# Attention with pooled queries and a three-way max FFN on one core: weights converted in two DVE passes ahead of the first FFN, key sums of eight units on PE, twelve score buffers

## The chip, the cores and the metric

The kernel runs on one core of one Trainium2 chip. The metric is the device time of one execution in microseconds (us), as the median of several runs. The engines named here are PE (matrix products), DVE (vector), ACT (scalar, activations and copies), POOL (elementwise) and SP (which issues nearly all DMAs). Each works through its own instructions strictly in the order in which the program puts them.

## The reference, cut to what matters

```python
q_pool = q.reshape(B, H, S // 2, 2, D).mean(axis=3)       # 8 x 8 heads, 1152 -> 576 queries, D = 64
scores = scale * np.matmul(q_pool, k.transpose(0, 1, 3, 2))  # 576 x 1152
scores = scores - np.max(scores, axis=-1, keepdims=True)
attn = np.exp(scores)
attn = attn / (np.sum(attn, axis=-1, keepdims=True) + 1e-09)
x = np.matmul(attn, v)                    # then to 4608 tokens x 512
h = np.maximum(np.maximum(x @ w1, x @ w2), x @ w3)        # 512 -> 768
out = h @ w_out                                           # 768 -> 512
```

q, k and v are float32. The four weight matrices arrive as float64, which the kernel reads as pairs of 32-bit words.

## The kernel before, in words

**Units.** A unit `d` (0 to 63) is one half (288) of the pooled queries of two heads; two units share one load of keys, queries and values. For each of nine blocks of 128 keys, PE makes the scores of both heads (`pqk`, from two parts of each operand: `qq`, `kc`), ACT copies them into a score buffer (`s`, three blocks in each), and DVE keeps the running maximum over blocks (`acc`). PE turns the maxima (`pmt`), DVE reduces them (`m`), PE spreads them (`pmb`), DVE subtracts them from the scores in six instructions, ACT takes the exponentials in six, and PE multiplies by the values (`pav`). ACT copies the product to `xr`, once per unit. A unit needs three score buffers; there are six.

**Key sums.** POOL adds the nine blocks of a unit's exponentials with eight instructions into `ksum` (lines 643 and 645). For the first 16 units six small PE products turn `ksum` into columns (`psum`, line 704), DVE inverts them, PE spreads the result (line 719) and DVE scales `xr` (line 728). Later units use another form (lines 687 to 697).

**FFN.** The tokens go in nine chunks, eight of 512 and one of 576 split in two. A chunk has 18 first-layer weight tiles in six groups of three. For each, PE makes twelve products (`ph`, line 935); ACT and DVE keep the maximum of three (`hm`), which is split into a high and a low part (`h_hi`, `h_lo`). The second layer (`po`, line 990) has 72 products. The chunk's work is mixed into that of the following units.

**Weights.** Each of 24 weight tiles (18 of the first layer, 6 of the second) is made from 128 x 512 float64 numbers: a DMA brings them to one of the two halves of `w64` (line 820); ACT scales the high words (line 835); four DVE passes rebuild the float32 value and the rest that it lacks (lines 838, 843, 848, 851); ACT makes the high part (line 862) and two more passes the low part (lines 865, 868). Even tiles go in one piece and leave the last two passes to POOL; odd tiles go in two pieces of 256 columns and have all six passes on DVE. The load of tile j waits until tile j-2 is done. During chunk 0 these tiles feed its products directly, and each of the 18 is stored to `w_split` in HBM (line 881), from which the later chunks fetch it (line 895). There are four tiles of room (`w`), so the first four conversions come among units 1 to 4, the fifth only when chunk 0 has used the first, and the second layer's six at the end of chunk 0.

**Order.** A planner in the program (`arrange`) puts all steps in order: it follows its own cost of every step, and among those ready on an engine it takes the one with the lowest urgency, from the tables `RANK` (by kind) and `NUDGE` (single steps of units and chunks below 20). Two PSUM buffers called `ff` serve `ph`, `po`, `psum`, the first eight units' `pav` and the conversion.

Of the kernel before, what the change touches and what calls it, by code (L numbers as in the profile page):

```python
# [18 lines left out]
P = 128  # L19
D = 64  # L20
# [16 lines left out]
    "qk": -364.0396,  # L37
    "cp": -126.5549,
    "mx": -318.2574,
    "rows": -969.9796,  # L40
    "red": -172.0313,
    "bc": -345.8464,
    "sub": 215.1752,
    "exp": 196.9402,
    "keys": -671.9276,
    "av": 14.8431,
    "xcopy": -516.1778,
    "psum": 398.4083,
    "eps": 343.2889,
    "inv": 357.0576,  # L50
    "xm": -706.0274,
    "load": 386.6538,
    "prep": 638.9001,
    "move": 1290.4425,
    "split": 283.1141,
    "ffn": -33.8173,
    "rate": 1.047,
    "mm": 49.0387,
    "fetch": 603.0832,
    "evac": -724.5554,  # L60
    "hhigh": 1228.3483,
    "hlow": -714.7034,
    "conv": 648.8915,
    "rate0": 4.5084,
    "first_qk": -97.1625,
    "first_cp": -630.79,
    "first_mx": 212.4188,
    "first_sub": 204.5779,
    "first_exp": 244.1512,
    "first_keys": -1118.9276,  # L70
    "first_av": 141.406,
    "first_xcopy": -152.0387,
    "first_psum": 65.359,
    "first_inv": 141.5566,
    "first_xm": 829.3378,
    "first_load": -197.5173,
    "first_prep": 180.1798,
    "first_move": -1436.3679,
    "first_split": 375.0794,
# [94 lines left out]
EARLY = 16  # L174
SPLIT = 8
IDLE = 0
APART = 0
SWITCH = 0.2


# [894 lines left out]
```

## Time and profile before

| What | us |
|---|---|
| three runs, median (lowest to highest) | 1474.91 (1472.44 to 1477.5) |
| the profiled execution, its own time | 1472.96 |
| its span, first to last instruction | 1471.1 |
| PE busy | 1398.0 |
| POOL busy | 1079.1 |
| DVE busy | 1044.0 |
| ACT busy | 902.5 |

A row of instructions in the profile reads: line, engine, operation, output and inputs by tile name, shapes, count, then busy time and the mean nanoseconds of one. A window row reads: from and to in us, its length, then the busy time of PE, PEld (weight loads, which run beside products), DVE, ACT and POOL with instruction counts, then the TensorE clock that was granted as a share of full speed, the mean busy share of the 16 DMA engines, and GB/s. A timeline row begins with its start and its length in us. SPq is the queue of SP.

### The profile page before, as it was taken

To read this page: it belongs to the slowest core of one execution; us is meant where nothing else is said; L and a number is where in the kernel's file an instruction comes from. 1 tells how busy PE (TensorE), PEld (TensorE's weight loads), DVE (VectorE), ACT (ScalarE), POOL (GpSimd) and SP (SyncE) were. 2 spreads that over 40 slices of the span, in tenths; PEclk is the share of its full clock that TensorE was granted. 3 is DMA by queue.
4 is the path that set the end of the run, shared out by engine and by line. 5 is a ranking of instruction groups with operands and counts; after the bars stand their busy time and mean duration, and the time that the engine had idled before them with its cause. 6 is when DMAs were issued, how large, how long until landed. Compare 5 with 4: busy or idle time off the path is not lost.

```text
span 1471.1 us, 24704 instructions
## 1 busy us (share of the span) xinstructions
PE 1398.0 (95%) x8704; PEld 1098.5 (75%) x8704; DVE 1044.0 (71%) x1441; ACT 902.5 (61%) x1464; POOL 1079.1 (73%) x835
## 2 busy tenths in 40 slices
PE   4888999898899999999999999999999999999999
PEld 4566677675677878777777777777777777878999
DVE  3897789898877767777688778777787768861110
ACT  3776776567666666567566766666766757651211
POOL 1897975889868878679888878888787978772210
PEclk9988999998899999999999999999999999999999
DMA  6675456576456656565567556664566556414441
GB/s 181 169 203 147 122 153 207 184 206 194 118 151 185 201 155 182 168 181 148 148 192 203 152 145 191 182 182 134 163 189 184 149 148 185 144 69 162 149 161 59
DMA packets 114762, 240.71 MB, mean 164 GB/s; under 512 B 15440, under 2 KB 75216, under 8 KB 114640
## 3 DMA queue, kind: packets, MB, share of 16 engines
q1 hardware_dynamic: 114064, 238.55, 55.8%
q8 instruction: 70, 1.15, 0.3%
q10 hardware_dynamic: 576, 0.59, 0.2%
q14 instruction: 52, 0.43, 0.1%
HBM read 144.70 MB, written 18.87 MB: 111 GB/s over the span
## 4 chain that ended last, share of the span: by engine, by line
PE 75%; DVE 10%; DMA 4%; ACT 4%; issue 4%; POOL 2%; SPq 1%; ACTq 0%; DVEq 0%; POOLq 0%
PE ph L935 28%; PE pav L673 14%; PE po L990 10%; PE pqk L542 9%; PE pqk L543 8%; DVE s L624 3%; DVE acc L557 3%; DMA kraw<-in_kT_dram 2%; PE pmt L593 2%; PE psum L687 2%; PE pmb L609 2%; POOL ksum L645 1%; ACT s L548 1%; DVE w L848 1%; DVE w L843 1%
## 5 line engine op out<-in xcount | busy, mean ns | idle before, releaser
L645 POOL TENSOR_TENSOR ksum<-ksum,s 128x576 f32<-128x576 f32 x448 | 638.2, 1425 | 26.1 <-ACT s L630 3.5
L935 PE MATMUL ph<-xh,w 128*128 128x512 f32 (+2 forms) x1440 | 464.3, 376 | 2.7 <-DVE w L868 1.3
L548 ACT COPY s<-pqk 128x576 f32<-128x576 f32 x576 | 362.4, 639 | 103.4 <-PE pqk L543 97.8
L624 DVE TENSOR_TENSOR s<-s,pmb 128x693 f32<-128x693 f32 (+1 forms) x384 | 395.1, 1049 | 39.5 <-PE pmb L609 38.3
L542 PE MATMUL pqk<-qq,kc 128*128 128x288 f32 x1152 | 357.9, 326 | 56.1 <-DVE acc L557 30.7
L557 DVE TENSOR_TENSOR acc<-acc,pqk 128x576 f32<-128x576 f32 x448 | 335.3, 749 | 82.8 <-ACT s L548 78.1
L630 ACT ACTIVATE s<-s 128x693 f32<-128x693 f32 (+1 forms) x384 | 352.5, 933 | 41.9 <-DVE s L624 38.6
L543 PE MATMUL pqk<-qq,kc 128*128 128x288 f32 x1152 | 332.3, 303 | 0.0
L542 PEld LDWEIGHTS pqk<-qq,kc 128*128 128x128 f32 x1152 | 225.6, 196 | 113.7 <-DVE acc L557 44.5
L673 PE MATMUL pav<-s,v 128*64 128x288 f32 x2304 | 306.8, 418 | 1.3 <-ACT s L630 1.0
L935 PEld LDWEIGHTS ph<-xh,w 128*128 128x128 f32 x1440 | 263.1, 188 | 41.4 <-ACT xr L682 1.8
L935 PE MATMUL ph<-xl,w 128*128 128x512 f32 (+2 forms) x720 | 268.3, 373 | 0.0
L673 PEld LDWEIGHTS pav<-s,v 128*64 128x64 f32 x2304 | 165.2, 140 | 119.3 <-issue 16.6
L543 PEld LDWEIGHTS pqk<-qq,kc 128*128 128x128 f32 x1152 | 227.5, 197 | 10.4
L643 POOL TENSOR_TENSOR ksum<-s 128x576 f32<-128x576 f32 x64 | 92.0, 1437 | 107.8 <-ACT s L630 104.8
L956 DVE TENSOR_TENSOR hm<-hm,ph 128x512 f32<-128x512 f32 (+2 forms) x120 | 75.8, 631 | 126.8 <-PE ph L935 124.8
L966 POOL TENSOR_TENSOR h_lo<-hm,h_hi 128x512 fp32r<-128x512 f32 (+2 forms) x60 | 70.6, 1176 | 126.1 <-ACT h_hi L963 123.6
L935 PEld LDWEIGHTS ph<-xl,w 128*128 128x128 f32 x720 | 135.8, 189 | 11.5
L438 POOL TENSOR_TENSOR kraw<-kraw 128x1152 fp32r<-128x1152 f32 x31 | 82.8, 2670 | 63.1 <-DMA qraw<-in_qT_dram 26.6
L599 DVE TENSOR_REDUCE m<-pmt 116x3 f32<-116x384 f32 (+1 forms) x128 | 61.3, 488 | 89.9 <-PE pmt L593 89.8
L682 ACT COPY xr<-pav 128x288 f32<-128x288 f32 x64 | 25.5, 399 | 147.0 <-PE pav L673 146.9
L694 DVE RECIPROCAL rs<-rs 128x288 f32<-128x288 f32 (+1 forms) x64 | 96.5, 1507 | 17.7 <-ACT rs L691 17.3
(57 smaller groups left out, 1293.6 us busy)
## 6 DMA issues: line engine op xcount, KB each, us to landing
w<-w_split SPq DMA_DIRECT2D x144, 512.0 KB, 3.6
kc<-kraw SPq DMA_DIRECT2D x384, 96.0 KB, 2.2
qq<-qraw SPq DMA_DIRECT2D x252, 144.0 KB, 3.3
v<-in_vr_dram SPq DMA_DIRECT2D x32, 576.0 KB, 3.8
kraw<-in_kT_dram SPq DMA_DIRECT2D x31, 576.0 KB, 6.0
qraw<-in_qT_dram SPq DMA_DIRECT2D x31, 576.0 KB, 4.0
w<-in_win_dram SPq DMA_DIRECT2D x18, 512.0 KB, 5.9
w_split<-w SPq DMA_DIRECT2D x18, 512.0 KB, 5.5
```

Of the source, the lines that this page charges most:

```text
L542: nc.tensor.matmul(ps[:, h - hs[0], :QH], w, qq[:, 0, h], start=True, stop=False)
L543: nc.tensor.matmul(ps[:, h - hs[0], :QH], w, qq[:, 1, h], start=False, stop=True)
L548: nc.scalar.copy(o.s[kk // 3][:, kk % 3, slice(*hs)], o.ps[kk, hs][:, :, :QH])
L557: nc.vector.tensor_tensor(acc, acc, ps, op=ALU.max)
L624: nc.vector.tensor_tensor(s, s, o.pb[h][:, None, :w].broadcast_to([P, 3, w]), op=ALU.subtract)
L630: nc.scalar.activation(s, s, AF.Exp, scale=SCALE)
L643: vec[e].tensor_tensor(o.ksum, o.s[0][:, 0], x, op=ALU.add)
L645: vec[e].tensor_tensor(o.ksum, o.ksum, x, op=ALU.add)
L673: nc.tensor.matmul(o.pav[64 * h : 64 * h + 64, :QH], pr.v[:, kk, h], o.s[kk // 3][:, kk % 3, h], start=(kk == 0), stop=(kk == NK - 1),)
L694: nc.vector.reciprocal(o.rs, o.rs)
L935: nc.tensor.matmul(t.ps[:, : hi - lo], w[:, a, kk], xx[:, kk, lo:hi], start=(kk == 0 and i == 0), stop=(kk == 3 and i == 2),)
L990: nc.tensor.matmul(t.ps[:, : hi - lo], ww[:, kk, ms], hh[:, kk, lo:hi], start=(kk == 0 and i == 0), stop=(kk == 5 and i == 2),)
```

## The change

1. **Conversion.** Only `shift` and `sign` stay on DVE, and every tile goes in one piece. The low words become a count of units of the last place in a new ACT pass (`units_of`), POOL adds it to the value as an integer (`carry`), ACT makes the high part, POOL the low part (`low`). Nothing of the odd tiles' last passes is left on DVE.
2. **Place.** All 24 conversions are planned at the head of chunk 0, not inside it. The 18 first-layer tiles are all stored to `w_split`, through the same four `w` buffers, and chunk 0 fetches them from there like the other chunks. Its first fetches wait until all 18 high parts are made.
3. **Key sums.** For units 0 to 7 POOL's eight adds go. PE multiplies each exponential block by a 128 x 32 block of ones into one of four 32-column tiles (18 products), ACT copies the result (`kt`), and three small products with a selection matrix give the columns.
4. **Buffers.** Eight score buffers in place of six, and units 0 to 7 put their last three blocks into four buffers that later hold the FFN's `h`, so that up to four units are held at once.
5. **Tables.** `RANK` and `NUDGE` have other numbers throughout; the scratch space of the DMA queue is set to 1024 bytes.

```diff
-    "sub": 215.1752,
+    "sub": 3142.3735,
...
-    "conv": 648.8915,
+    "conv": 1789.7153,
...
-    spool = ctx.enter_context(tc.tile_pool(name="spool", bufs=6))
+    spool = ctx.enter_context(tc.tile_pool(name="spool", bufs=THIRDS))
...
-    hpool = ctx.enter_context(tc.tile_pool(name="hpool", bufs=1))
+    hpool = ctx.enter_context(tc.tile_pool(name="hpool", bufs=4))
...
-                if kk % 3 == 0 and old2:
-                    after += [old2.avs[kk + 2], old2.sums[kk + 1]]
+                if kk % 3 == 0:
+                    lent = d < LENT and kk == 6
+                    seq = homes[lent]
+                    past = len(seq) - (4 if lent else THIRDS)
+                    if past >= 0:
+                        was, last_kk = seq[past]
+                        after += [was.avs[last_kk], was.sums[last_kk - 1] if was.sums else chain[was.d]]
+                    seq.append((o, kk + 2))
...
-        for kk in range(1, NK):
+        for kk in range(1, NK) if d >= SUMS else ():
...
+        def columns_keys(e):
+            o.psm = ps_ff.tile([P, 512], F32, tag="ff", name=f"psum{d}")
+            for kk in range(NK):
+                for h in range(2):
+                    t = 2 * h + kk % 2
+                    nc.tensor.matmul(
+                        o.psm[32 * t : 32 * t + 32, :QH],
+                        ones[:, :32],
+                        o.s[kk // 3][:, kk % 3, h],
+                        start=kk < 2,
+                        stop=kk >= NK - 2,
+                        tile_position=(0, 32 * t),
+                    )
+
+        def sums_copy(e):
+            o.kt = small.tile([P, QH], F32, tag="kt", name=f"kt{d}", bufs=1)
+            nc.scalar.copy(o.kt, o.psm[:, :QH])
+
+        def sums_turn(e):
+            for i in range(3):
+                nc.tensor.matmul(
+                    o.psm[:96, QH + 2 * i : QH + 2 * i + 2], o.kt[:, 96 * i : 96 * i + 96], sel, start=True, stop=True
+                )
...
-            wide = j % 2 == 1
-            m = DM // 2 if wide else DM
+            m = DM
...
-                def power(e):
-                    nc.vector.tensor_scalar(q.m.bitcast(U32), q.f, 0xFF800000, None, op0=ALU.bitwise_and)
-
-                def rest(e):
-                    nc.vector.scalar_tensor_tensor(
-                        q.low.bitcast(F32), q.low, 2.0**-52, q.m, op0=ALU.mult, op1=ALU.mult
-                    )
+                def units_of(e):
+                    nc.scalar.activation(o.low, o.low, AF.Copy, scale=2.0**-29)
+
+                def carry(e):
+                    nc.gpsimd.tensor_tensor(o.f, o.f, o.low, op=ALU.add)
...
-                a = cstep([dve(m)], power, [a])
-                a = cstep([dve(m)], rest, [a], give=None if wide else "ff")
-                end = dve(m) if wide else pool(m)
-                c = cstep([end], low, [c, a])
-                return cstep([end], total, [c, a], give="ff" if wide else None)
+                a = cstep([dve(m)], sign, [a], give="ff")
+                c = cstep([act(m)], units_of, [loaded])
+                a = cstep([pool(m)], carry, [a, c])
+                c = cstep([("act", 0.09 + m / 1200)], high, [a] + gone + highs[-1:])
+                highs.append(c)
+                return cstep([pool(m)], low, [c, a])
...
-            gone = wuse[j - 4] if 4 <= j < NG else []
+            gone = [stored[j - 4]] if 4 <= j < NG else []
...
-            if b:
-                fetch(g)
-            else:
+            fetch(g)
+
+        base = NG * b
+        if b == 0:
+            for g in range(NG + 6):
                 convert(g)
```

Three places show what this does to the order. The first is DVE at the conversion of weight tile 5, which before stands between units 10 and 11 (`w64` with two numbers after it is a PSUM piece, `w0_5` the finished tile):

```order
L838 TENSOR_SCALAR w64_105<-w64_5_0_1947 128x256
L843 SCALAR_TENSOR_TENSOR w64_5_0_1947<-w64_5_0_1947,w64_105 128x256
L838 TENSOR_SCALAR w64_105<-w64_5_256_1952 128x256
L848 TENSOR_SCALAR w64_5_0_1947<-w64_5_0_1947 128x256
L843 SCALAR_TENSOR_TENSOR w64_5_256_1952<-w64_5_256_1952,w64_105 128x256
L851 SCALAR_TENSOR_TENSOR w64_105<-w64_105,w64_5_0_1947 128x256
L848 TENSOR_SCALAR w64_5_256_1952<-w64_5_256_1952 128x256
L865 TENSOR_TENSOR w64_5_0_1947<-w64_5_0_1947,w0_5_1957 128x256
L851 SCALAR_TENSOR_TENSOR w64_105<-w64_105,w64_5_256_1952 128x256
L868 TENSOR_TENSOR w0_5_1957<-w64_5_0_1947,w64_105 128x256
L865 TENSOR_TENSOR w64_5_256_1952<-w64_5_256_1952,w0_5_1957 128x256
L599 TENSOR_REDUCE m10_0_1987<-pmt10_0_1967 116x3
```

In the change tiles 7 and 8 stand on DVE between units 4 and 5, before unit 4's maxima are reduced:

```order
L574 TENSOR_TENSOR acc4_831<-acc4_831,pqk4_7_928 128x576
L777 TENSOR_TENSOR xr_108<-xr_108,psum2_834 128x288
L890 TENSOR_SCALAR w64_107<-w64_7_0_960 128x512
L895 SCALAR_TENSOR_TENSOR w64_107<-w64_7_0_960,w64_107 128x512
L574 TENSOR_TENSOR acc4_831<-acc4_831,pqk4_8_955 128x576
L890 TENSOR_SCALAR w64_107<-w64_8_0_1000 128x512
L895 SCALAR_TENSOR_TENSOR w64_107<-w64_8_0_1000,w64_107 128x512
L622 TENSOR_REDUCE m4_0_1023<-pmt4_0_1005 116x3
```

So DVE has two rows for a tile where it had twelve (or four for an even tile), and they have moved from the units beside chunk 0 to the units before it. By the place of the rows, tile 17 is made about unit 9.

The second place is PE around the sums of unit 3. Before, one row of six small products stands among unit 5's scores:

```order
L673 MATMUL pav4_1007<-s4_0_732,v2_635 64x288 x6
L542 MATMUL pqk5_5_1019<-qq2_1_728,kc2_1_587 128x288
L543 MATMUL pqk5_5_1019<-qq2_1_728,kc2_1_587 128x288
L704 MATMUL psum3_1025<-ones_99,ksum3_823 96x1 x6
L542 MATMUL pqk5_6_1039<-qq2_1_728,kc2_2_663 128x288
```

In the change:

```order
L556 MATMUL pqk5_0_963<-qq2_1_739,kc2_0_433 128x288
L740 MATMUL psum3_972<-s3_0_571,ones_99 32x288 x6
L740 MATMUL psum3_972<-s3_1_667,ones_99 32x288 x6
L740 MATMUL psum3_972<-s3_2_714,ones_99 32x288 x6
L616 MATMUL pmt4_0_1005<-ident_94,acc4_831 116x128 x3
L616 MATMUL pmt4_1_1012<-ident_94,acc4_831 116x128 x2
```

Eighteen products with 288 columns now stand right ahead of the turning of unit 4's maxima, and the three small products that close the sum follow after `pmb` of unit 4.

The third place is SP at the end of the first-layer conversions, in the change alone (`w64` is a load, `w_split` a store, `w0_0` and `w0_1` the first tiles fetched for chunk 0):

```order
L423 DMA kraw6_1941<-in_kT_dram 128x1152
L875 DMA w64_107<-in_wout_dram 128x1024
L428 DMA qraw6_1946<-in_qT_dram 128x1152
L926 DMA w_split<-wc16_1915 128x1024
L940 DMA w0_0_1961<-w_split 128x1024
L940 DMA w0_1_1970<-w_split 128x1024
L476 DMA kc6_0_1997<-kraw6_1941 64x384 x3
L875 DMA w64_107<-in_wout_dram 128x1024
L926 DMA w_split<-wc17_1952 128x1024
```

The fetch of `w0_0` waits for the high part of tile 17, and the moves of the seventh pair's keys (`kc6`) are queued behind it.

More of the change, by code (lines that the diff above doesn't have):

```diff
@@ L36 @@
 RANK = {
[L37 to L42, printed above, removed]
-    "sub": 215.1752,
[L44 to L62, printed above, removed]
-    "conv": 648.8915,
[L64 to L79, printed above, removed]
+    "qk": -1510.4874,
+    "cp": 341.719,
+    "mx": -1025.8335,
+    "rows": -1076.2425,
+    "red": -548.2463,
+    "bc": -1262.927,
+    "sub": 3142.3735,
+    "exp": 525.325,
+    "keys": -2302.3792,
+    "av": 993.0292,
+    "xcopy": -1532.5591,
+    "psum": 894.5822,
+    "eps": -283.5976,
+    "inv": 2643.9912,
+    "xm": 734.8097,
+    "load": -1080.9686,
+    "prep": 2513.6067,
+    "move": 1636.3282,
+    "split": -554.6463,
+    "ffn": 799.8325,
+    "rate": 3.2243,
+    "mm": 890.9148,
+    "fetch": 352.4738,
+    "evac": -1545.3662,
+    "hhigh": 1511.8456,
+    "hlow": -1944.9353,
+    "conv": 1789.7153,
+    "rate0": 0.2997,
+    "first_qk": -303.4192,
+    "first_cp": 676.4114,
+    "first_mx": 1216.1884,
+    "first_sub": 1650.8042,
+    "first_exp": 104.7791,
+    "first_keys": -3781.1847,
+    "first_av": -649.9138,
+    "first_xcopy": 1333.1821,
+    "first_psum": 1828.5982,
+    "first_inv": -371.7508,
+    "first_xm": -316.0721,
+    "first_load": -2349.1886,
+    "first_prep": 520.6971,
+    "first_move": -389.7336,
+    "first_split": 1846.5518,
 }
 NUDGE = {
[81 rows of a table removed]
[88 rows of a table added]
 }
@@ L174 @@
 EARLY = 16
+THIRDS = 8
+LENT = 8
+SUMS = 8
 SPLIT = 8
@@ L340, in tile_attention_ffn @@
     nc.vector.memset(eps, EPS)
+    sel = cpool.tile([P, 2], F32, name="sel")
+    nc.vector.tensor_tensor(sel, ident[:, ::64], ident[:, 32::64], op=ALU.add)
     wo_hi = cpool.tile([P, 6, DM], F32R, name="wo_hi")
@@ L522, in scores @@
         o = units[d] = Job()
-        o.n, o.half = n, half
+        o.n, o.half, o.d = n, half, d
         pr = pairs[n]
@@ L546, in copy @@
                     if kk % 3 == 0:
-                        o.s[kk // 3] = spool.tile([P, 3, 2, QH], F32, tag="s", name=f"s{d}_{kk // 3}")
+                        if d < LENT and kk == 6:
+                            s = hpool.tile([P, 3, NQ], F32, tag="t", name=f"s{d}_2")
+                            o.s[2] = s.rearrange("p k (h q) -> p k h q", h=2)
+                        else:
+                            o.s[kk // 3] = spool.tile([P, 3, 2, QH], F32, tag="s", name=f"s{d}_{kk // 3}")
                     nc.scalar.copy(o.s[kk // 3][:, kk % 3, slice(*hs)], o.ps[kk, hs][:, :, :QH])
@@ L750, in values @@
         if early:
-            t = chain[d] = step("psum", d, [pe(1020)], columns, [o.sums[-1], a], cols=100, mode=1, take="ff")
+            if d < SUMS:
+                t = chain[d] = step("keys", d, [pe(2300)], columns_keys, [a], cols=5184, mode=2, take="ff")
+                t = step("eps", d, [("act", 0.4)], sums_copy, [t])
+                t = step("psum", d, [pe(300)], sums_turn, [t], cols=10, mode=1)
+            else:
+                t = chain[d] = step("psum", d, [pe(1020)], columns, [o.sums[-1], a], cols=100, mode=1, take="ff")
             t = step("inv", d, [("dve", 0.1)], add_eps6, [t, spreads.get(d - 2)])
@@ L803, in tile_attention_ffn @@
     converted, stored = {}, {}
+    highs = []
     def ffn(b, d):
@@ L831, in rebias @@
                     q.ps = ps_ff.tile([P, 512], F32, tag="ff", name=f"w64_{j}_{x}")
-                    q.m = q.ps[:, 512 - m :]
-                    q.low, q.ff = o.low[:, cut], q.ps[:, :m] if wide else o.ff[:, cut]
-                    q.f = q.ff.bitcast(U32)
-                    nc.scalar.activation(q.m, o.ff[:, cut], AF.Copy, scale=REBIAS)
+                    q.m = q.ps[:, :m]
+                    nc.scalar.activation(q.m, o.ff, AF.Copy, scale=REBIAS)
                 def shift(e):
                     nc.vector.tensor_scalar(
-                        o.f[:, cut], q.m.bitcast(U32), 3, 0x7FFFFFFF, op0=ALU.logical_shift_left, op1=ALU.bitwise_and
+                        o.f, q.m.bitcast(U32), 3, 0x7FFFFFFF, op0=ALU.logical_shift_left, op1=ALU.bitwise_and
                     )
@@ L855, in high @@
+                def carry(e):
+                    nc.gpsimd.tensor_tensor(o.f, o.f, o.low, op=ALU.add)
                 def high(e):
                     if j < NG:
-                        if j not in wt:
-                            wt[j] = wpool.tile([P, 2, NPAIR, P], F32R, tag="w", name=f"w{b}_{j}")
-                        o.hi, o.lo = (wt[j][:, i].rearrange("p c m -> p (c m)") for i in range(2))
+                        o.t = wpool.tile([P, 2, NPAIR, P], F32R, tag="w", name=f"wc{j}")
+                        o.hi, o.lo = (o.t[:, i].rearrange("p c m -> p (c m)") for i in range(2))
@@ L860, in high @@
                     else:
                         o.hi, o.lo = wo_hi[:, j - NG], wo_lo[:, j - NG]
-                    nc.scalar.copy(o.hi[:, cut], q.ff)
+                    nc.scalar.copy(o.hi[:, cut], o.ff)
                 def low(e):
-                    vec[e].tensor_tensor(q.ff, q.ff, o.hi[:, cut], op=ALU.subtract)
-                def total(e):
-                    vec[e].tensor_tensor(o.lo[:, cut], q.ff, q.low.bitcast(F32), op=ALU.add)
-                a = cstep([act(m)], rebias, [loaded] + gone, take="ff")
+                    nc.gpsimd.tensor_tensor(o.lo[:, cut], o.ff, o.hi[:, cut], op=ALU.subtract)
@@ L871, in part @@
+                a = cstep([act(m)], rebias, [loaded], take="ff")
                 a = cstep([dve(m)], shift, [a])
-                a = cstep([dve(m)], sign, [a])
-                c = cstep([("act", 0.09 + m / 1200)], high, [a])
-                a = cstep([dve(m)], power, [a])
-                a = cstep([dve(m)], rest, [a], give=None if wide else "ff")
-                end = dve(m) if wide else pool(m)
-                c = cstep([end], low, [c, a])
-                return cstep([end], total, [c, a], give="ff" if wide else None)
+                a = cstep([dve(m)], sign, [a], give="ff")
@@ L902, in begin @@
         def begin():
-            h.hi = hpool.tile([P, 6, NQ], F32R, tag="h_hi", name=f"h_hi{b}")
-            h.lo = hpool.tile([P, 6, NQ], F32R, tag="h_lo", name=f"h_lo{b}")
+            third = lambda name: hpool.tile([P, 3, NQ], F32, tag="t", name=f"{name}{b}").bitcast(F32R)
+            quarters = [third(f"h{i}") for i in range(4)]
+            h.hi, h.lo = quarters[:2], quarters[2:]
         def supply(g):
-            if b:
-                fetch(g)
-            else:
+            fetch(g)
+        base = NG * b
+        if b == 0:
+            for g in range(NG + 6):
                 convert(g)
-                fetched[g] = converted[g]
-        base = NG * b
         for g in range(4):
@@ L962, in high @@
                         def high(e, f=f, o=o, lo=lo, hi=hi):
-                            nc.scalar.copy(h.hi[:, f, lo:hi], o.x)
+                            nc.scalar.copy(h.hi[f // 3][:, f % 3, lo:hi], o.x)
                         def low(e, f=f, o=o, lo=lo, hi=hi):
-                            vec[e].tensor_tensor(h.lo[:, f, lo:hi], o.x, h.hi[:, f, lo:hi], op=ALU.subtract)
+                            vec[e].tensor_tensor(
+                                h.lo[f // 3][:, f % 3, lo:hi], o.x, h.hi[f // 3][:, f % 3, lo:hi], op=ALU.subtract
+                            )
                         x = ffn_step("hhigh", at, n, [("act", 0.09 + m / 1200)], high, [prev[w0]])
@@ L975, in ffn @@
         if b == 0:
-            for g in range(NG, NG + 6):
-                convert(g)
             hdone += [c for i in range(NG, NG + 6) for c in converted[i]]
```

17 lines of the change are left out of this document (10 added, 7 removed), and 169 rows, old and new, of the table NUDGE.

## The prediction

> **What bounds the kernel now.** I first cut the span at 45, 182, 401 and 1325 us, close to the copies of `xr` of units 0, 8, 18 and 63, and read the window view over these stages:
>
> ```profile
> core 0: us, PE busy (x) PEld busy (x) DVE busy (x) ACT busy (x) POOL busy (x), PEclk, DMA share, GB/s
> 0.00:45.00 45.00, 24.58 (x103) 19.23 (x103) 20.41 (x31) 20.78 (x31) 12.22 (x14) 0.96 0.65 172
> 45.00:182.00 137.00, 120.41 (x848) 85.59 (x848) 116.18 (x184) 100.08 (x155) 122.44 (x89) 0.91 0.60 164
> 182.00:401.00 219.00, 193.66 (x1223) 147.15 (x1221) 198.96 (x352) 149.56 (x253) 173.57 (x132) 0.92 0.60 178
> 401.00:1325.00 924.00, 916.55 (x5638) 710.24 (x5637) 688.18 (x838) 605.42 (x966) 743.32 (x572) 1.00 0.57 165
> 1325.00:1471.00 146.00, 142.77 (x900) 136.25 (x898) 20.32 (x37) 26.68 (x60) 27.58 (x31) 1.00 0.40 134
> ```
>
> From 401 us on PE is busy 99% of the time at full clock: PE is the bound, and only PE work could change that part. Before 401 it isn't. In **stage 1** (45 to 182, eight units, 17.1 us each) PE idles 17 us, its clock is granted at 0.91, and POOL is the busiest. In **stage 2** (182 to 401, ten units and chunk 0's first layer) PE idles 25 us at a clock of 0.92, and DVE is the busiest with 91%. The chain of waits, restricted to the two stages, names who ended last (I quote the columns that a row gives):
>
> ```profile
> by line: PE pav L673 18.0%; POOL ksum L645 12.5%; issue 11.7%; DVE acc L557 11.7%; DVE s L624 9.5%; PE pqk L542 8.1%; PE pqk L543 5.7%; DMA w<-in_win_dram 3.3%; ACT s L548 2.1%; POOL ksum L643 2.0%; ACT s L630 1.9%; PE pmt L593 1.8%; PE psu
> by line: issue 12.8%; DVE s L624 12.6%; DVE acc L557 9.9%; DVE w L848 5.3%; DVE w L843 5.1%; ACT s L548 4.9%; DVE w L851 4.7%; PE ph L935 4.3%; DVE w L838 4.0%; ACT s L630 3.9%; PE pqk L542 3.4%; PE pav L673 3.0%; PE po L990 2.9%; DVE acc L
> ```
>
> Stage 1 is mixed: PE, POOL's key sums (14.5%) and DVE take turns. Stage 2 is DVE's, and four conversion passes (lines 838, 843, 848, 851) are 19% of its chain, some 42 us.
>
> **How much PE work there is.** Full-clock steps tell what a stage could cost if PE never waited:
>
> ```profile
> 429.23 0.29 PE L542 MATMUL pqk<-qq,kc 128*128 128x288 f32 x1
> 429.37 0.29 PE L543 MATMUL pqk<-qq,kc 128*128 128x288 f32 x1
> 429.59 4.59 PE L673 MATMUL pav<-s,v 128*64 128x288 f32 x36
> 434.10 0.54 PE L593 MATMUL pmt<-ident,acc 128*116 128x128 f32 x3
> 435.48 0.40 PE L935 MATMUL ph<-xl,w 128*128 128x512 f32 x1
> 435.71 0.39 PE L935 MATMUL ph<-xh,w 128*128 128x512 f32 x1
> 185.96 1.18 PE psum L704 x12
> ```
>
> Score products start 0.135 us apart, so 36 take 4.8 us; `pav` takes 4.5; an FFN product 0.23; the column products 1.18, and I put the other small ones at 2.2 together, an estimate: five `pmt` at 0.14, five `pmb` alike, and 0.8 for the spreading, which is as many products as the columns. A unit is 12.7 us. Stage 2 holds ten units and some 240 FFN products (55 us): 182 us of work, of which the last units lack some `psum`; I use 178. It took 219. So stage 2 can lose at most about 41 us. Stage 1 holds 102 us of work in 137.
>
> **Conversion and its place.** The instructions that touch a weight tile, by engine (DVE, then ACT, then POOL), in stages 1 and 2:
>
> ```profile
> 45.00:182.00 137.00, 15.50 (x32) 0.91 0.60 164
> 182.00:401.00 219.00, 72.23 (x160) 0.92 0.60 178
> 45.00:182.00 137.00, 5.80 (x12) 0.91 0.60 164
> 182.00:401.00 219.00, 29.05 (x60) 0.92 0.60 178
> 45.00:182.00 137.00, 4.72 (x4) 0.91 0.60 164
> 182.00:401.00 219.00, 23.50 (x20) 0.92 0.60 178
> ```
>
> ```profile
> L838 DVE TENSOR_SCALAR w<-w 128x512 uint32<-128x512 uint32 x12 | 8.2, 687 | 2.5 <-ACT w L835 2.2
> L843 DVE SCALAR_TENSOR_TENSOR w<-w,w 128x512 uint32<-128x512 uint32 x12 | 8.2, 684 | 0.1
> L835 ACT ACTIVATE w<-w 128x512 f32<-128x512 f32 x12 | 7.8, 652 | 6.7 <-DVE hm L956 4.5 <-DMA w<-in_wout_dram 1.4 <-DMA w<-in_win_dram 0.7
> L862 ACT CAST w<-w 128x512 fp32r<-128x512 f32 x9 | 6.1, 676 | 4.5 <-DVE w L843 4.4
> L682 ACT COPY xr<-pav 128x288 f32<-128x288 f32 x64 | 25.5, 399 | 147.0 <-PE pav L673 146.9
> L865 POOL TENSOR_TENSOR w<-w,w 128x512 f32<-128x512 f32 x9 | 11.7, 1305 | 2.3 <-ACT w L862 2.3
> L868 POOL TENSOR_TENSOR w<-w 128x512 fp32r<-128x512 f32 x9 | 9.4, 1043 | 0.2
> ```
>
> Four tiles are converted in stage 1 and twenty in stage 2; by the order about 17 will be in stage 1 and 7 in stage 2. A tile will cost DVE 0.687 + 0.684 = 1.37 us. ACT gets three passes; `units_of` (integers to integers) isn't in the trace, and neither is POOL's integer add: I take ACT's 0.65 and POOL's 1.3 from the nearest rows, between half and twice the row for both (17 tiles at twice would add 11 us to ACT and 22 to POOL, in stage 1). So ACT 1.98 and POOL 1.3 + 1.3 = 2.6 a tile.
>
> - Stage 2, DVE: 198.96 - 72.23 + 7 x 1.37 = 136 us. ACT: 149.56 - 29.05 + 14 = 134. POOL: 173.57 - 23.50 + 18 = 168. None of them fills 182 us, so PE's 178 becomes the bound. From 401 on PE fills 99%; here I allow 96%, for the first fetches and the six last tiles: **185 us in place of 219, a gain of 34**.
> - Stage 1, DVE: 116.18 - 15.50 + 17 x 1.37 = 124. ACT: 100.08 - 5.80 + 17 x 1.98 = 128, and with eight `kt` copies of the shape of the `xr` copy, 0.4 each, it is 131.
>
> **Key sums.** POOL's two rows in stage 1, from the groups of that window:
>
> ```profile
> L645 POOL TENSOR_TENSOR ksum<-ksum,s 128x576 f32<-128x576 f32 x58 | 82.3, 1420 | 4.4 <-ACT s L630 1.3
> L643 POOL TENSOR_TENSOR ksum<-s 128x576 f32<-128x576 f32 x8 | 11.4, 1420 | 5.7 <-ACT s L630 5.7
> ```
>
> POOL falls from 122.44 by 93.7 and 4.72 and gains 17 x 2.6 = 44: 68 us, no bound any more. PE pays. The 18 products with 32 columns have `pav`'s 288 columns and its count, so 4.5 us is the upper end. The lower end comes from how `pav` runs:
>
> ```profile
> L673 PE MATMUL pav<-s,v x2304: 403/406/742, 38.5 to 1324.8; 128*64 128x288 f32 x192
> L542 PE MATMUL pqk<-qq,kc x1152: 288/295/609, 13.0 to 1303.9; 128*128 128x288 f32 x192
> ```
>
> With the same 288 columns a `pav` instruction stays 0.11 us longer than a score product, so each seems to stream about twice, yet the next starts after 0.125: two column tiles run beside each other. Four would need 2.25. I take 2.5, by this row and a little for entering and leaving the mode. The three turning products are half of line 704's count, 0.6. Per unit 2.5 + 0.6 - 1.18 = 1.9, in all **15 us on PE in stage 1** (13 to 31), where PE idles 17 and holds 102 + 15 = 117 us of work.
>
> [...]
>
> **Score buffers.** Copies that wait for `ksum` to free a buffer are small already:
>
> ```profile
> ACT s L548 <- POOL ksum L645: 0.5, 1, 0.5
> PE pqk L542 <- DVE acc L557: 12.1, 17, 2.0
> ```
>
> (stage 1's waits: total, times, longest). What PE waits for is DVE's maxima, which stand behind other DVE work. Twelve buffers allow scores further ahead; I count nothing for it by itself, but expect three engines at 117 to 131 us to need it. Below, 0 to 7 us of gain.
>
> **Stage 1 in sum.** ACT 131, DVE 124, PE 117 at full clock. An engine can be filled to 99% for a while:
>
> ```profile
> 50.00:75.00 25.00, 20.90 (x140) 13.77 (x140) 24.72 (x39) 20.04 (x33) 21.09 (x16) 1.00 0.58 156
> 75.00:100.00 25.00, 20.51 (x138) 15.19 (x132) 24.71 (x47) 19.44 (x32) 24.53 (x19) 0.80 0.68 203
> ```
>
> With ACT at 95%, stage 1 takes **138 us in place of 137**: POOL's 94 us are exchanged, not saved. Range 130 to 150.
>
> **DMA.** Thirteen more loads and stores of 0.52 MB in stage 1 are 13.6 MB, 99 GB/s beside 164. The busiest 25 us of before moved 240 GB/s at a share of 0.78:
>
> ```profile
> 325.00:350.00 25.00, 22.12 (x156) 16.46 (x155) 24.10 (x43) 20.50 (x40) 20.21 (x18) 0.98 0.78 240
> ```
>
> So I estimate 0.86: not full, but landings get later, which is the first rival. Chunk 0's fetches, 9.4 MB, go into stage 2, where 20 loads and stores fall to 7.
>
> **After 401.** PE's work is the same there; its 7.5 us of idle time may close or double with the new tables. I count 0.
>
> **Sum.** +1 - 34 = -33 on a span of 1471.1: 1438. The execution took 1.9 us more than its span, so 1440; the median of the runs is 2 above the profiled one: **1442**.
>
> **Rivals.**
>
> *The conversion loop sets the pace (A).* Tile j is loaded only when j-2 is done. Loads before:
>
> ```profile
> 209.56 0.33 SPq L820 DMA_DIRECT2D w<-in_win_dram  x1
> 327.73 0.91 SPq L820 DMA_DIRECT2D w<-in_wout_dram  x2
> w<-in_win_dram SPq DMA_DIRECT2D x18, 512.0 KB, 5.9
> ```
>
> From tile 6 to tile 18 are six rounds of 19.7 us for two tiles. The new round is 5.9 of landing, 0.65 + 1.37 + 1.3 + 0.65 + 1.3 of passes, 11 us, and its waits in four queues; I expect 15 to 16, so that tile 16 is loaded at 44 + 8 x 15.5 = 168 and chunk 0 starts about 185. If it stays 19.7, that is 34 us later, which eats the gain: 1476, no change. For it: DMA at 0.86. Against it: 5 us of DVE passes per tile gone.
>
> *Slower (B).* The same loop decides from 20 us on: each further us costs 8. At 22 us, when loads or stores land 3 us later and ACT, whose copies of scores are queued behind a pass that waits, loses as much, the time is 1442 + 8 x 6.5 = 1494.
>
> *Key sums two at a time (C).* 4.5 us a unit: PE holds 133 us in stage 1, which then takes about 148: 1452.
>
> *More overlap (D).* Twelve buffers and a warm clock bring stage 1 to 126 and stage 2 to 178: 1423 or less.
>
> **How the numbers follow.** Forecast (1430 to 1458, C's 1452 lies in it): 0.62 with C. D (1405 to 1430): 0.16. A: 0.12, of which 0.08 within 0.3% of before (1470.5 to 1479.3) and 0.04 below. B: 0.10, of which 0.02 still counts as no change. About 0.3% is what a measurement of this kernel can tell from no change. Faster 0.82, same 0.10, slower 0.08. The range takes most of D and reaches into A: 1408 to 1474; about 0.18 is left out.
>
> **What would show it.** Right: unit 18's `xr` copy near 372 us, DVE under 75% and PE over 95% in the ten units before, line 838's successors in stage 1; 18 column products in 2.5 us. Wrong: ACT idle before its conversion pass by a DMA, `ph` starting after 200 us, the PE clock still at 0.9 between units 9 and 18, or new idle time after 400 us.

## The result, and the profile after

| What | before | after |
|---|---|---|
| four runs each, median (lowest to highest), us | 1473.68 (1471.57 to 1477.5) | 1451.01 (1447.02 to 1453.69) |
| ratio after to before, 95% interval | | 0.9841 [0.9807, 0.9875] |
| span of the profiled execution, us | 1471.1 | 1447.3 |

The change makes the kernel 1.6% faster: 24 us on the span, where 33 were predicted. These are the windows of the changed kernel, cut near the same copies of `xr` (units 0, 8, 18 and 63), with the columns of before:

```profile
45.00:201.00 156.00, 139.19 (x1098) 93.29 (x1096) 124.86 (x190) 129.03 (x208) 78.63 (x63) 0.92 0.77 231
201.00:401.00 200.00, 194.51 (x1313) 152.47 (x1311) 142.84 (x208) 137.29 (x217) 165.75 (x126) 0.99 0.63 183
401.00:1292.00 891.00, 883.52 (x5488) 686.90 (x5484) 675.49 (x831) 599.27 (x955) 732.40 (x563) 1.00 0.58 168
1292.00:1447.00 155.00, 152.13 (x942) 144.04 (x940) 20.32 (x37) 27.87 (x62) 32.04 (x37) 1.00 0.38 130
```

**Stage 2 came as foretold**: PE is busy 97% at a clock of 0.99, DVE 71%. The stage is 200 us instead of 219, and it holds more: the two rows below are `ph` and `po` of before up to unit 18, the next two those of the change (busy time, and the records in brackets).

```profile
0.00:405.60 405.60, 56.64 (x216) 0.92 0.60 171
0.00:405.60 405.60, 6.64 (x27) 0.92 0.60 171
```

```profile
0.00:401.45 401.45, 62.74 (x231) 0.96 0.69 200
0.00:401.45 401.45, 19.24 (x72) 0.96 0.69 200
```

That is 60 FFN products more, 14 us at 0.23 each. At equal work stage 2 takes 186 us; 185 were predicted.

**Stage 1 didn't**: 156 us, where 137 were before and 138 were predicted. The engine sums behind that 138 were nearly right for DVE (124.9 for 124) and ACT (129.0 for 131); POOL had 78.6 for 68, half of the stage. What is wrong is how full the stage runs. ACT is busy 83% of it, not 95%, and PE again idles 17 us, though it has more to do.

The new operations, in the timeline of PE for one unit and in the groups of that stage:

```profile
45.34 2.62 PE L740 MATMUL psum<-s,ones 128*32 128x288 f32 x36
49.05 0.59 PE L755 MATMUL psum<-sel,kt 128*96 128x2 f32 x6
```

```profile
L903 POOL TENSOR_TENSOR w<-w 128x512 uint32<-128x512 uint32 x18 | 18.7, 1041 | 20.2 <-DVE w L895 9.0 <-ACT s L565 8.5 <-ACT xr L705 2.7
L900 ACT ACTIVATE w<-w 128x512 uint32<-128x512 uint32 x18 | 12.4, 688 | 1.5 <-DMA w<-in_win_dram 1.4
```

A block of key sums takes 2.62 us (2.5 predicted), its turn 0.59 (0.6), the pass `units_of` 0.69 (0.65), the integer add 1.04 (1.3). The tile loop, from the load of the first two tiles to that of tile 16, and the first product of chunk 0:

```profile
43.34 0.90 SPq L875 DMA_DIRECT2D w<-in_win_dram  x2
183.65 0.53 SPq L875 DMA_DIRECT2D w<-in_win_dram  x1
209.24 0.63 PE L980 MATMUL ph<-xh,w 128*128 128x512 f32 x1
```

Eight rounds in 140.3 us are 17.5 each (15 to 16 predicted), and chunk 0 starts at 209, not 185.

In sum, between the exact marks and with the FFN products put where they were before: up to unit 8's copy +18 us, units 8 to 18 -36, the rest -6. Two questions follow. Why did stage 1 not take up PE's new work? And which of the change's parts earns the gain?

### The profile page after: what moved, and what is told of

It reads as the page before. It is cut to its first block, busy times and chain, and to the rows that moved or that the text cites. A ratio compares the mean times of both kernels' runs of the same rounds, so it can differ in the third digit from the quotient of the medians.

```text
span 1447.3 us, 24926 instructions
## 1 busy us (share of the span) xinstructions
PE 1394.7 (96%) x8944; PEld 1096.1 (76%) x8944; DVE 984.6 (68%) x1298; ACT 914.1 (63%) x1472; POOL 1014.9 (70%) x795
## 4 chain that ended last, share of the span: by engine, by line
PE 78%; DMA 6%; DVE 4%; ACT 4%; issue 3%; POOL 3%; SPq 2%; ACTq 0%; DVEq 0%; POOLq 0%
PE ph L980 28%; PE pav L696 16%; PE po L1035 10%; PE pqk L555 9%; PE pqk L556 8%; DMA kraw<-in_kT_dram 2%; PE psum L710 2%; PE pmt L616 2%; DVE acc L574 2%; PE pmb L632 2%; DMA qq<-qraw 2%; ACT s L565 1%; DMA w<-in_win_dram 1%; ACT s L653 1%; POOL ksum L668 1%
## 5 line engine op out<-in xcount | busy, mean ns | idle before, releaser
L668 POOL TENSOR_TENSOR ksum<-ksum,s 128x576 f32<-128x576 f32 x392 | 557.6, 1422 | 22.5 <-ACT s L653 3.6
L647 DVE TENSOR_TENSOR s<-s,pmb 128x1035 f32<-128x1035 f32 (+1 forms) x384 | 396.4, 1046 | 42.5 <-PE pmb L632 42.4
L653 ACT ACTIVATE s<-s 128x1035 f32<-128x1035 f32 (+1 forms) x384 | 355.7, 933 | 55.1 <-DVE s L647 49.4
L555 PE MATMUL pqk<-qq,kc 128*128 128x288 f32 x1152 | 348.3, 319 | 42.6 <-DVE acc L574 20.9
L556 PE MATMUL pqk<-qq,kc 128*128 128x288 f32 x1152 | 326.4, 300 | 0.0
L696 PE MATMUL pav<-s,v 128*64 128x288 f32 x2304 | 302.5, 414 | 0.8 <-DVE w L895 0.4
L555 PEld LDWEIGHTS pqk<-qq,kc 128*128 128x128 f32 x1152 | 221.7, 192 | 105.7 <-DVE acc L574 41.4
L556 PEld LDWEIGHTS pqk<-qq,kc 128*128 128x128 f32 x1152 | 223.2, 194 | 9.3
L666 POOL TENSOR_TENSOR ksum<-s 128x576 f32<-128x576 f32 x56 | 80.5, 1438 | 116.9 <-ACT s L653 116.8
L1011 POOL TENSOR_TENSOR h<-hm,h 128x512 fp32r<-128x512 f32 (+2 forms) x60 | 70.6, 1176 | 110.4 <-ACT h L1008 110.4
L1035 PE MATMUL po<-h,wo_hi 128*128 128x512 f32 (+2 forms) x480 | 141.2, 378 | 0.0
```

Of the source, the lines that this page charges most:

```text
L555: nc.tensor.matmul(ps[:, h - hs[0], :QH], w, qq[:, 0, h], start=True, stop=False)
L556: nc.tensor.matmul(ps[:, h - hs[0], :QH], w, qq[:, 1, h], start=False, stop=True)
L647: nc.vector.tensor_tensor(s, s, o.pb[h][:, None, :w].broadcast_to([P, 3, w]), op=ALU.subtract)
L653: nc.scalar.activation(s, s, AF.Exp, scale=SCALE)
L666: vec[e].tensor_tensor(o.ksum, o.s[0][:, 0], x, op=ALU.add)
L668: vec[e].tensor_tensor(o.ksum, o.ksum, x, op=ALU.add)
```

## Experiments on stage 1: the order kept, work taken out or added

The planner's costs, and with them the order, stay as they are in these kernels; only what some instructions process, or how many of them a step holds, is changed. Each was run once, and the change's own four runs lie between 1447.02 and 1453.69 us, so a total inside that range tells nothing by itself. "Stage 1" is from unit 0's copy of `xr` to unit 8's, "stage 2" from there to unit 18's. For before and the change these are 135.95 and 222.25 us, and 156.30 and 199.65. A run of before beside them took 1472.24 us (fewer key products, no loads, narrow ACT, narrow DVE) or 1471.38 (the others); the change's profiled run took 1449.06.

**Key sums on PE doubled.**

```diff
-            for kk in range(NK):
+            for kk in [*range(NK), *range(NK)]:
```

> The changed kernel in its own order, with the 18 products of each key sum made twice (the second pass starts afresh), 2.6 us more of PE in each of eight units, 21 in all. Theory B (PE's order takes the stage): stage 1 grows from 156 by 15 to 21 us. Theory A2: PE has some room, so it grows by less than 8.

1461.51 us. The windows of its stage 1, of all of PE and of tile `psum` alone, and behind them the same two of the change:

```profile
47.64:221.84 174.20, 156.89 (x1387) 101.31 (x1386) 125.38 (x189) 130.49 (x210) 79.35 (x64) 0.95 0.70 208
47.64:221.84 174.20, 50.81 (x720) 0.95 0.70 208
```

```profile
45.50:201.80 156.30, 139.49 (x1099) 93.59 (x1092) 124.84 (x189) 129.78 (x209) 79.35 (x64) 0.92 0.77 230
45.50:201.80 156.30, 31.96 (x432) 0.92 0.77 230
```

`psum` grows by 18.9 us and the stage by 17.9. PE's idle time, length less busy time, is 17.3 us; it was 16.8. So at this order what PE is given in addition comes on top.

**Four of the 18 key products left.**

```diff
-            for kk in range(NK):
+            for kk in range(2):
...
```

> The changed kernel in its own order, with 4 of the 18 products of the key sums in units 0 to 7 (the sums are wrong). That takes some 2.0 us of PE from each of eight units, 16 in all. Theory A: PE has idle time in stage 1, so stage 1 (156 us) falls by less than 6 us. Rival, PE's key sums fill stage 1: it falls by 12 to 16 us.

1452.34 us, no gain. Its stage 1, by the same two windows:

```profile
47.72:208.65 160.93, 135.00 (x877) 91.66 (x875) 124.94 (x189) 129.57 (x209) 79.38 (x64) 0.85 0.75 223
47.72:208.65 160.93, 17.27 (x208) 0.85 0.75 223
```

`psum` falls by 14.7 us, yet the stage takes 4.6 longer. The granted clock was 0.85 in place of 0.92, PE's other products were busy for 117.7 us in place of 107.5 (each run's PE row less its `psum` row), and PE idles 26 us in place of 17; no run shows why it idles more. The two results together forbid calling stage 1 simply PE-bound: more PE work lengthened it, less didn't shorten it.

**No loads of `w64` but the first two.**

```diff
-                nc.sync.dma_start(o.w.rearrange("p n t -> p (n t)"), dram.bitcast(U32))
+                if j < 2:
+                    nc.sync.dma_start(o.w.rearrange("p n t -> p (n t)"), dram.bitcast(U32))
```

> The changed kernel in its own order, but only the first two of the 24 weight tiles are loaded; the other 22 are made from what lies in w64 (their values are wrong). The changed kernel took 156 us from the xr copy of unit 0 to that of unit 8 (stage 1) and its first ph came at 209 us. Theory A (the loop of load, passes and next load sets the pace, and engines stand at conversion passes that wait for it): stage 1 falls to 136 to 144 us, the first ph comes before 195, the span falls by 12 to 20 us. Rival, the added work on ACT, DVE and PE fills the stage: stage 1 stays above 150 and the span within 5 us of 1447.

1440.7 us. Stage 1 takes 154.13 us (-2.2), and the first `ph` starts at 207.3, where it started at 209.2. Rival A, whose loop waits for its loads, falls. The 8 us by which it is under the change's profiled run come mostly after unit 18; a single run can't say more on them.

**The low-word pass `units_of` on ACT on 8 of 512 columns**, with a zero in place of its result:

```diff
-                    nc.scalar.activation(o.low, o.low, AF.Copy, scale=2.0**-29)
+                    nc.scalar.activation(o.low[:, :8], o.low[:, :8], AF.Copy, scale=2.0**-29)
...
```

> The changed kernel in its own order, where the new ACT pass (units_of) covers 8 of 512 columns and POOL adds zero in place of its result (the rest beyond the high words is lost). That takes some 0.6 us of ACT from each of 24 tiles, 11 us in stage 1. Theory A: it is in the loop only beside the DVE passes, so stage 1 falls by less than 5 us. Rival, ACT fills stage 1 (129 of 156 us busy): it falls by 9 to 12 us.

1449.87 us, stage 1 156.36, with ACT at 122.77 us in place of 129.78. The stage doesn't follow ACT's total.

**Both DVE passes on 8 columns.**

```diff
-                        o.f, q.m.bitcast(U32), 3, 0x7FFFFFFF, op0=ALU.logical_shift_left, op1=ALU.bitwise_and
+                        o.f[:, :8], q.m[:, :8].bitcast(U32), 3, 0x7FFFFFFF, op0=ALU.logical_shift_left, op1=ALU.bitwise_and
...
```

> The changed kernel in its own order, where both DVE passes cover 8 of 512 columns (weights are wrong). That takes 1.2 us of DVE from each of 24 tiles, 22 us in stage 1, and shortens each round of the loop by as much. Theory A: the round shrinks by 1.2 us for each of some eight rounds, so stage 1 falls by 6 to 12 us. Rival, DVE fills stage 1 (125 of 156 us busy): it falls by 18 to 22 us.

1447.11 us, stage 1 155.52, with DVE at 107.59 us in place of 124.84. The fall of 0.8 us is far under what either theory gave.

**All of it at once**: the loads gone, and the passes of ACT, DVE and POOL ahead of the high part on 8 columns.

> The changed kernel in its own order, with every pass of the conversion on ACT and DVE and the integer add on POOL on 8 of 512 columns, except the making of the high and low parts, and with only two of 24 loads (weights are wrong). That takes about 1.2 us of DVE, 1.2 of ACT and 1.0 of POOL from each tile, and the landing of the loads, all at once. Theory A2 (conversion passes cost stage 1 its 20 us, but only together: where one is taken away another stands in its place): stage 1, 156 us in the changed kernel, falls to 142 or less. Theory B (the units' own instructions and the key sums in this order, with PE at the clock it is granted, take the stage: PE is busy 139 of 156 us): stage 1 stays at 150 to 156.

1436.75 us. Its stages 1 and 2:

```profile
47.22:195.85 148.63, 136.93 (x1099) 91.35 (x1097) 107.41 (x189) 113.94 (x210) 64.16 (x64) 0.94 0.63 186
195.85:394.30 198.45, 194.29 (x1312) 151.99 (x1311) 137.14 (x208) 131.06 (x216) 160.56 (x125) 0.99 0.57 168
```

With 15 to 17 us of the conversion's work gone from each of three engines, and the loads gone, 8 of the 20 added us leave stage 1. That lies between the two theories (142 or less, 150 or more), so neither holds as it was put: the passes are a part of the 20 us, together, and the larger part stays. The first `ph` still starts at 202.1, so the conversion loop is no more than a part of the reason for the late chunk 0. DVE, ACT and POOL, all under 80% busy here, don't set the stage's length by their totals. What PE waits for most in the change is the same as before; its largest wait in stage 1, before and after (total, times, longest):

```profile
PE pqk L542 <- DVE acc L557: 10.9, 14, 2.0
```

```profile
PE pqk L555 <- DVE acc L574: 9.4, 13, 1.9
```

These are turnarounds: scores wait until DVE has taken the maxima of earlier ones, behind whatever stands ahead of that on DVE. They are over half of PE's 17 us of idle time in both kernels.

## Experiments on before: does less work free the stages there?

**Before, part of the DVE conversion on 8 columns**, in both stages (one of four such places):

```diff
-                    nc.vector.tensor_scalar(q.m.bitcast(U32), q.f, 0xFF800000, None, op0=ALU.bitwise_and)
+                    nc.vector.tensor_scalar(q.m[:, :8].bitcast(U32), q.f[:, :8], 0xFF800000, None, op0=ALU.bitwise_and)
```

> The kernel before in its own order, with the DVE passes shift, power and (in even tiles) sign and (in odd tiles) the first pass of the low part on 8 columns (weights are wrong). That takes about 46 of DVE's 72 us of conversion from stage 2 (xr of unit 8 to xr of unit 18, 222 us before). If DVE's conversion passes pace stage 2, as the prediction has it: it falls by 25 to 40 us. Rival, they are hidden behind other work: by less than 10.

1463.3 us. Stage 2 of before, and of this run:

```profile
183.35:405.60 222.25, 196.91 (x1249) 148.63 (x1249) 200.69 (x354) 148.59 (x253) 176.81 (x135) 0.92 0.59 176
```

```profile
182.13:400.14 218.01, 197.98 (x1251) 149.62 (x1250) 173.59 (x354) 148.41 (x254) 176.83 (x135) 0.91 0.61 179
```

27 us of DVE work are gone and the stage is 4 us shorter. That speaks against the step "DVE paces stage 2", if the order is kept. The run was expected to take 46 from it: a pass on 8 columns still takes 0.16 to 0.17 us in it, and 42 us of conversion stay on DVE, which this run doesn't test.

**Before, POOL's key sums of units 0 to 7 on 4 of 288 columns** in seven adds of eight:

```diff
-                    vec[e].tensor_tensor(o.ksum, o.ksum, x, op=ALU.add)
+                    z = 4 if d < 8 else QH
+                    vec[e].tensor_tensor(o.ksum[:, :, :z], o.ksum[:, :, :z], x[:, :, :z], op=ALU.add)
```

> The kernel before in its own order, where seven of eight of POOL's key-sum adds in units 0 to 7 cover 4 of 288 columns of each head (the sums are wrong). That takes about 75 us of POOL from stage 1 (136 us before). If POOL paces stage 1 together with its in-order neighbours: it falls by 10 to 20 us. Theory B, carried to the kernel before (the order of the units on PE, ACT and DVE takes it): by less than 5.

1469.05 us. Stage 1 of before, and of this run:

```profile
47.40:183.35 135.95, 119.36 (x840) 85.29 (x840) 114.67 (x182) 100.49 (x155) 121.39 (x89) 0.91 0.59 160
```

```profile
47.73:183.93 136.20, 119.40 (x833) 84.82 (x834) 114.66 (x182) 100.54 (x155) 61.32 (x87) 0.90 0.59 161
```

POOL's busy time is halved, and the stage takes 0.3 us more. POOL's 14.5% of the chain of waits was no price: with those sums nearly gone, the stage ends at the same time by other instructions.

So at a kept order neither kernel gives back more than a part of what is taken out. What a part of the change is worth beyond that has to come through another order, and the tables make the order. They have to be fitted anew for each combination of parts.

## Experiments with fitted tables: which part earns the gain

Four kernels, each with `RANK` and `NUDGE` found by the same search over orders: (1) before, unchanged; (2) before with the new conversion only, still inside chunk 0, key sums on POOL, six score buffers; (3) that with the conversion ahead of chunk 0; (4) the complete change. (2) and (3) are made from the change, and keep from it that `h` lies in four buffers instead of two, and the scratch space of the DMA queue. Their line numbers differ by a few, since the tables have other lengths.

For (1) the diff holds numbers alone:

```diff
-    "sub": 215.1752,
+    "sub": 229.579366771,
...
```

> The kernel before with its own conversion, place, key sums and buffers; only the numbers in RANK and NUDGE are others, found by a longer search over orders. Theory 'order alone' (the change gains because its tables are better, not by its parts): this run falls by as much as the change did, to about 1451 us. Theory 'two DVE passes' (the conversion as written is what lets a good order exist): the old conversion keeps DVE at about 199 us of work in stage 2, no order can hide it, and this run stays at 1460 to 1470, stage 2 at 215 to 222 us.

For (2), against the change, beside the tables:

```diff
-THIRDS = 8
-LENT = 8
-SUMS = 8
+THIRDS = 6
+LENT = 0
+SUMS = 0
...
-            gone = [stored[j - 4]] if 4 <= j < NG else []
+            gone = wuse[j - 4] if 4 <= j < NG else []
...
-            fetch(g)
+            if b:
+                fetch(g)
+            else:
+                convert(g)
+                fetched[g] = converted[g]
...
-        if b == 0:
-            for g in range(NG + 6):
-                convert(g)
...
+            for g in range(NG, NG + 6):
+                convert(g)
```

> Only the new conversion (two DVE passes, whole tiles): it stays inside chunk 0 as before, key sums are POOL's in all units, six score buffers, none lent; tables fitted to this by the same search. Theory 'two DVE passes': at least as fast as the change, 1430 to 1450 us, with stage 1 back at about 136 us since the key sums' 17.5 us of PE are gone. Theory 'place' (the conversions have to be out of chunk 0): 1455 or more, since the first FFN products wait for POOL and ACT passes again. Theory 'buffers': 1455 or more, with POOL's key sums and six buffers holding stage 2 at 215 or more.

For (3), against the change, beside the tables; (4) differs from the change in the numbers of the tables alone:

```diff
-THIRDS = 8
-LENT = 8
-SUMS = 8
+THIRDS = 6
+LENT = 0
+SUMS = 0
```

> The run with only the new conversion, and its place ahead of chunk 0 as in the change; key sums on POOL, six buffers; tables fitted to this. Theory 'two DVE passes': within 7 us of the run with the conversion alone, to either side. Theory 'place': faster than that by 10 or more. POOL then has key sums (94 us) and the adds of 17 tiles (40 us) in stage 1, so a stage 1 of 145 to 155 us, paid back in stage 2.

> The change complete (key sums of 8 units on PE, 12 buffers), tables fitted by the same search. Theory 'two DVE passes': 1430 to 1445, within 8 us of the run with the conversion alone; key sums on PE cost their 15 us in stage 1 and give back about as much by POOL's free time. Theory 'buffers and key sums': faster than the conversion alone and than the conversion ahead by 10 us or more. If key sums on PE only cost, slower than the conversion alone by 10 or more.

| kernel | us, median (lowest to highest) | ratio to before, 95% interval |
|---|---|---|
| before (beside these four) | 1473.27 (1469.77 to 1477.35) | 1 |
| (1) before, fitted | 1462.33 (1459.7 to 1464.8) | 0.9929 [0.9903, 0.9956] |
| (2) new conversion only, fitted | 1431.03 (1429.63 to 1434.14) | 0.9720 [0.9695, 0.9745] |
| (3) and ahead of chunk 0, fitted | 1432.48 (1430.25 to 1438.75) | 0.9721 [0.9694, 0.9748] |
| (4) complete change, fitted | 1434.62 (1430.42 to 1436.65) | 0.9738 [0.9710, 0.9765] |
| the change with its own tables | 1451.01 (1447.02 to 1453.69) | 0.9841 [0.9807, 0.9875] |

**The new conversion is enough.** Tables alone bring 11 us; the new conversion, with tables fitted to it, another 31. Its place ahead of chunk 0, the key sums on PE and the added score buffers add nothing that shows: the intervals of (2), (3) and (4) lie on one another. And (2), with the fewest edits, beats both kernels of this study: 42 us under before, and its interval lies wholly under that of the change. The same holds for (4), which differs from the change in numbers alone: about 1% of the time was left in the tables. No run has the other parts with the old conversion, or the four `h` buffers alone, so these runs don't show that only the new conversion could do it.

(1) came as the theory "two DVE passes" had it: with the old conversion DVE stays 92% busy in stage 2, and the stage takes 222 us with the fitted tables too, for 3 FFN products more than in before.

```profile
185.40:407.40 222.00, 202.51 (x1283) 152.96 (x1284) 204.68 (x359) 153.15 (x258) 176.91 (x135) 0.92 0.61 183
```

The stages, between the exact copies of `xr` (units 0 to 8, 8 to 18, and for (2) also 18 to 63 and the end), first of (2), then (3), then (4). The profiled execution of (3) took 1438.75 us, 6 over the median:

```profile
51.65:188.30 136.65, 121.52 (x832) 85.40 (x832) 108.04 (x160) 102.66 (x158) 127.93 (x95) 0.89 0.57 156
188.30:411.80 223.50, 215.86 (x1396) 169.16 (x1397) 167.33 (x242) 165.06 (x264) 201.26 (x157) 0.97 0.66 199
411.80:1281.30 869.50, 869.47 (x5438) 680.02 (x5437) 666.20 (x821) 592.31 (x947) 728.49 (x563) 1.00 0.57 167
1281.30:1429.20 147.90, 144.58 (x907) 137.75 (x907) 20.30 (x37) 27.28 (x61) 29.05 (x31) 1.00 0.38 134
```

```profile
47.20:204.20 157.00, 134.19 (x852) 93.49 (x852) 123.16 (x185) 122.15 (x192) 145.48 (x112) 0.84 0.65 196
204.20:409.75 205.55, 201.47 (x1332) 158.57 (x1333) 146.73 (x214) 142.67 (x226) 179.78 (x137) 0.97 0.69 204
```

```profile
51.50:196.20 144.70, 129.65 (x1064) 87.19 (x1060) 122.62 (x185) 124.99 (x205) 76.62 (x61) 0.95 0.80 241
196.20:401.45 205.25, 201.85 (x1354) 158.52 (x1352) 147.08 (x211) 139.50 (x220) 169.34 (x130) 0.98 0.62 186
```

In (2) stage 1 is as long as in before, and so, at first sight, is stage 2; but its PE is busy 97% of the time where before had 89%, at 0.97 instead of 0.92, and the FFN products done by unit 18 have risen from 243 to 362:

```profile
0.00:411.80 411.80, 79.32 (x290) 0.94 0.63 183
0.00:411.80 411.80, 18.10 (x72) 0.94 0.63 183
```

119 products at 0.23 are 27 us: the stage gained 26, as work done and not as an earlier mark. Unit 0's copy comes 4 us later than before, so 21 us at equal work are gained up to unit 18. Another 21 came behind unit 18, where I had counted nothing. PE's idle time there fell from 10.7 us (924 and 146 less 916.55 and 142.77, in the prediction's rows) to 3.4, and a score product is busy for less in the mean. Tile `pqk` behind unit 18, in before and in (2):

```profile
405.60:1471.10 1065.50, 286.44 (x1604) 1.00 0.55 161
```

```profile
411.80:1429.20 1017.40, 274.01 (x1576) 1.00 0.54 163
```

That is 0.179 and 0.174 us a record, 7 us in all. Turning the maxima (`pmt`) accounts for 5 more of the 21 (40.38 us for 225 records before, 35.08 for 222). (1) shows that most of these 21 us need no new conversion: its units from 18 on took 13 us less than before's, by the tables alone. Of the distance from (1) to (2), at equal work, 22 us lie up to unit 18 and 8 behind it. In (2) the last conversion pass on DVE starts at 349 us, so nothing is converted there, and no run tells whether those 8 come from the order or from the `h` buffers.

(3) and (4) say what the key sums on PE are good for. With the conversion ahead of chunk 0 and the key sums on POOL, POOL has 145 us of work in stage 1 and the stage takes 157; with the key sums on PE, and the buffers, it takes 144.7. Since unit 0's copy comes 4 us later there, unit 8's is 8 us earlier, and part of that may be the 6 us by which the profiled execution of (3) is over its median. So they mend at most a load that the moved conversion itself brought, and leave the total where (2) had it.

What stays open: which property of the new conversion pays, DVE's shorter work, the shorter sequence of passes or the tiles in one piece. No run separates these. Each search may also have missed an order that is some us better, so differences of a few us among (2) to (4) mean nothing.

## Why the prediction was right or wrong

The time was within the forecast's own range (1430 to 1458), with luck: unit 8 came 17 us later than forecast, what follows it was 8 us better, and the errors partly cancel. That 1451 is also rival C's 1452 is chance, since C's cause didn't occur.

- **Stage 1, "+1": wrong, and this is the step that failed.** It read PE's 17 us of idle time as room for the key sums' 15, and let ACT be filled to 95%, on two 25 us windows in which DVE was full. The size of the key sums was nearly right (PE's `psum` grew from 14.45 to 31.96 us, 17.5). It also set PE's work at 117 us, at full clock; at the 0.92 that was granted PE was busy 139 us, which with 17 us of waits is the 156. PE's idle time in that stage is for the most part a wait inside each unit, for DVE's maxima, and was 15 to 18 us in all but four of the kernels here, whether PE was busy 119 or 157 us; (3) and the run with fewer key products had more (23 and 26), those with the conversion narrowed on three engines (12) or, in before, on DVE (14) less. At the change's own order added PE time came on top, as the doubled key sums show (18.9 us of products, 17.9 of stage). That taking it out gave nothing back is explained only in part: the clock was 0.85 in place of 0.92, and `pqk` and `pav` were busy 9 us longer. In the fitted order of (4) unit 8's copy comes 6 us earlier than in the change, so some of the 20 us belongs to the tables.
- **Stage 2, "-34": right in size** (36 at equal work, between the exact marks), and PE became its bound as said. The reason was too short. That PE fills the stage once DVE's conversion passes leave fails at a kept order (4 us for 27 of DVE). With the old conversion, fitted tables left the stage at 222 us with DVE 92% busy; with the new one it takes 223.5 and holds 27 us more of FFN work. So the new conversion pays through an order that uses it.
- **After 401 us, "0":** -6 at equal work in the change, -21 in (2). "Only PE work could change that part" overlooked that the order moves PE's idle time there (10.7 us in before, 6.4 in (1), 3.4 in (2)) and the mean busy time of a score product (0.179 and 0.174 us in before and (2)).
- **Unit 18's copy "near 372 us":** it came at 401.5. Of the 29 us, 19 are stage 1's and 14 the FFN products pulled forward; a start 2 us earlier and stage 2's 2 us beyond the forecast take some back.
- **Conversion round, "15 to 16 us":** 17.5. A load landed after 4.7 us in the median, sooner than the 5.9 of before, at a DMA share of 0.77 (0.86 estimated), so by subtraction what was sized too low are the waits of the passes in their four queues. Chunk 0's start at 209 was one of the prediction's own signs of being wrong.
- **Key sums, 2.5 and 0.6 us:** 2.62 and 0.59. Rival C (4.5) falls. One product of a block is recorded with 0.409 us in the mean and its weight load with 0.109; one after another the 36 products would take 14.7 us and the 36 loads 3.9, and both pass in the same 2.62 us, so here they run beside one another. The 0.25 us that the prediction added to its 2.25 for entering and leaving the mode was an estimate, and no run shows that cost by itself. With the key sums doubled, 72 products took 5.04 us: 36 more cost 2.42, which leaves 0.20 of the 2.62 for all else in a block.
- **Rival A:** the round was slower than forecast and chunk 0 began at 209, but without the loads it began at 207, so the landings don't set the pace. **B** didn't occur. Of **D**'s gain in stage 2 (41 us) 36 came; its stage 1 (126) didn't.

## What to carry to other kernels

Idle time of an engine in a stage is room only if its waits can move; look at what ends them (here mostly a turnaround inside each unit), and count added work there at its full price until an experiment says otherwise. In a program whose order is fitted to its work, taking work out at a kept order measures how well that work was covered, and not what its absence is worth: 27 us of DVE gave 4 in stage 2, while the new conversion, which takes 48 from DVE there, gave 26 with a fitted order. And when a change has several parts and new tables, fit the tables for each part alone before crediting any: here one part was enough, the simplest version was as fast as any, and 11 us belonged to the tables of before.

## What the runs showed of the hardware that was not expected

The granted clock of PE was lowest in the two stages 1 in which PE idled most: 0.85 in the run with four key products (busy 84%) and 0.84 in (3) (busy 85%). In the former `pqk` was busy for 62.8 us of stage 1 and `pav` for 50.4, against 58.1 and 45.8 in the change, with nearly the same counts. These 9 us are part of why it gained nothing. The busy share doesn't settle the clock: with PE busy 89% of stage 1 it was 0.89 in (2) and 0.96 in the change with narrow DVE passes, so the 0.95 with doubled key sums (busy 90%) shows nothing beside the change's 0.92 (89%). Each of these is one execution, so a link between work taken out and a lower clock is not shown here.

The integer add on POOL cost no more for being one: 1.04 us for 512 columns, as much as the cheaper of before's two float passes of that shape (line 868, 1043 ns), under the dearer (line 865, 1305 ns) from which I had sized it.
